# Combining weights of the last batch moved from among the experts to among the output's blocks, and four output blocks in column halves instead of five

## The chip, the cores and the metric

The kernel runs on one NeuronCore of one Trainium2 chip. A core has a matrix engine (TensorE, "PE" in the profile; its weight loads are "PEld"), a vector engine (VectorE, "DVE"), a scalar engine (ScalarE, "ACT"), GpSimd ("POOL"), and SyncE ("SP"), from which this kernel issues all its DMAs. The DMAs run on 16 DMA engines. The metric is the device time of one execution in microseconds; lower is better. The median of three runs is shown, and one more execution was taken with the hardware profiler.

## The reference

Causal attention with a decay per token (8 batches, 8 heads, 576 tokens, 64 channels a head) gives a matrix x of 4608 tokens by 512 channels. A soft mixture of experts follows: 32 slots, four for each of 8 experts. Cut to what matters here:

```python
logits = x @ phi                                   # 4608 x 32
d = exp(logits - logits.max(0)); d /= d.sum(0) + 1e-9    # over all tokens
slot_input = (d.T @ x).reshape(8, 4, 512)
for e in range(8):
    slot_out[e] = maximum(slot_input[e] @ w1[e], 0.0) @ w2[e]
c = exp(logits - logits.max(1)); c /= c.sum(1) + 1e-9    # over the 32 slots
out = c @ slot_out.reshape(32, 512)                # 4608 x 512
```

The weights d need every token's logits, so the experts can't start before the last batch's attention is done. The weights c, called combining weights here, need only their own token's logits, and they are needed only in the last line. Batches 0 to 6 have theirs made during the attention; this document is about those of batch 7 (`B - 1`, named `b` in the code).

## The kernel before, in words

The program is one long hand-ordered list. Every engine executes its own instructions in the order in which the Python code issues them, and semaphores hold an instruction back until its operands are ready. Nothing is reordered afterwards: a line of Python that stands earlier stands earlier in its engine's queue.

The attention takes the first 320 us or so. Then come, in this order:

1. The weights d of the last batch, and the slot inputs.
2. The experts, in the loop over `STEPS`. A step `(e, 0)` is expert e's first layer (`mlp1`, 32 matmuls, line 936) and `relu`; a step `(e, 4)` or `(e, 6)` is one half of its second layer (`mlp2`, line 973). The expert weights come from HBM in quarters of 512 KB each. 23 of the 64 quarters have a place of their own; the others go into memory that becomes free, so the weights stream in until near the end of the experts (line 128, function `wload`). For experts 4 to 7 the second layer is stored by output columns: steps `(e, 4)` give columns 0 to 255 of the slots' outputs, steps `(e, 6)` columns 256 to 511.
3. The output. `blocks(m, c)` makes block m, 512 tokens by the columns c: 8 matmuls of `cT` (combining weights, transposed) with `SO` (slot outputs, as a rounded part and a remainder), four copies from PSUM to a staging buffer, two on ACT and two on DVE (line 1053), and two DMAs to HBM from SP (line 1055). The first carries what ACT copied, the second what DVE copied. There are nine blocks. The first `FIRST` blocks are made in column halves, because columns 0 to 255 of the slot outputs are ready first: their blocks are written while `mlp2(e, 1)`, the last halves of the second layers, still run. A block in halves is four DMAs of 256 KB with runs of 1 KB in HBM; a whole block is two DMAs of 512 KB. `gathered`, `slots` and `halve` turn the sum of one column half of the expert outputs into `SO`.

The combining weights of batch 7 are made in these steps, which the change moves:

- `tokens(b, 0)`: the logits are turned to tokens-by-slots on PE (lines 457 and 458).
- `combine(b, 0)`: on DVE the maximum over the slots and the difference (lines 510 and 511); `combine(b, 1)`: the exponential on ACT (line 514); `combine(b, 2)`: on DVE the sum, the reciprocal and the product (lines 518 to 521).
- `split(3, 0)` and `split(3, 1)`: the rounded part on ACT (line 702) and the remainder on DVE (line 704), for batches 3 and 7 together.
- `cols(3, turn)`: five transposes on PE (line 712), and two casts on ACT into `cT` (line 718). They fill columns 864 to 1151 of `cT`, and block m reads columns 128 m to 128 m + 127, so the blocks 6, 7 and 8 need them.

PSUM banks are handed out in turn from a list named `ring` (function `turn`); before the second column half it has eight banks. The six staging buffers (`stage`) are used in turn too, one for each half block and two for a whole block.

Of the kernel before, what the change touches and what calls it, by code (L numbers as in the profile page):

```python
# [29 lines left out]
NQ = 8 * NE  # L30
QW = 1024
DEFER = 4
FIRST = 5

STEPS = (
    (0, 0), (1, 0), (2, 0), (3, 0), (0, 4), (0, 6), (1, 4), (1, 6), (4, 0), (5, 0), (2, 4), (2, 6), (3, 4), (3, 6),
# [36 lines left out]
def attn_softmoe(ctx: ExitStack, tc: tile.TileContext, qk, v, f, phi, w1, w2, cst, out):  # L73
# [86 lines left out]
    def batch(b):  # L160
        return 0 <= b < B
# [5 lines left out]
    def turn():  # L167
        ring.append(ring.pop(0))
        return ring[-1]
# [281 lines left out]
    def tokens(b, *ns):  # L451

        if not batch(b):
            return
        pm = turn() if b == B - 1 else scratch(False, f"tk{b}")
        for n in ns:
            nc.tensor.transpose(pm[:, 160 * n : 160 * n + 128], (LG, EX)[n][:, 0:128], ident)
            nc.tensor.matmul(pm[:, 160 * n + 128 : 160 * n + 160], (LX, EX[:, 128:256])[n], srep[:, 0:NS], start=True, stop=True)
        if 0 in ns:
            st["tok", b] = pm  # L460
            if b < B - 1:
                nc.tensor.transpose(pm[:, 160:192], st["mb", b][0:32, 1:2].broadcast_to([32, P]), ident[0:32, 0:32])
        if 1 in ns:
            nc.vector.tensor_copy(LD, pm[:, 160:320].rearrange("p (t s) -> p t s", t=NBLK))
# [36 lines left out]
    def combine(b, step):  # L501

        if not batch(b):
            return
        ce = ctok[:, b]
        if step == 0:

            lt = (TK if b < B - 1 else st["tok", b])[:, 0 : NBLK * NS].rearrange("p (t s) -> p t s", t=NBLK)
            sm = st["sm", b] = const.tile([P, 2, NBLK], F32, name=f"sm{b}", tag="sm", bufs=1)
            nc.vector.tensor_reduce(sm[:, 0], lt, axis=AX.X, op=ALU.max)  # L510
            nc.vector.tensor_tensor(ce, lt, wide(sm[:, 0]), op=ALU.subtract)
        elif step == 1:
            st["ce"] = turn()
            nc.scalar.activation(st["ce"][:, 0 : NBLK * NS].rearrange("p (t s) -> p t s", t=NBLK), ce, AF.Exp)
        else:
            sm, pm = st["sm", b], st["ce"]
            et, to = pm[:, 0 : NBLK * NS].rearrange("p (t s) -> p t s", t=NBLK), pm[:, NBLK * NS : NBLK * NS + NBLK]
            nc.vector.tensor_reduce(to, et, axis=AX.X, op=ALU.add)
            nc.vector.tensor_scalar_add(sm[:, 1], to, EPS)
            nc.vector.reciprocal(sm[:, 1], sm[:, 1])  # L520
            nc.vector.tensor_tensor(ce, et, wide(sm[:, 1]), op=ALU.mult)
# [174 lines left out]
    def split(b, *parts):  # L696

        if 0 in parts:
            CW[b] = tp.tile([P, NBLK, 2, 2, NS], F32R, name=f"cw{b}", tag="cw", bufs=2)
        hi, lo = (CW[b][:, :, :, r].rearrange("p t h s -> p h t s") for r in range(2))  # L700
        if 0 in parts:
            nc.scalar.copy(hi, ctok[:, b::4])
        if 1 in parts:
            nc.vector.tensor_tensor(lo, ctok[:, b::4], hi.bitcast(F32), op=ALU.subtract)

    def cols(b, bank):

        for lo, hi in ((0, 2), (2, 5)):
            pm = bank()
            for t in range(lo, hi):  # L710
                n = 128 if t < 4 else 64
                nc.tensor.transpose(
                    pm[:, 128 * (t - lo) : 128 * (t - lo) + n], CW[b][0:n, t].rearrange("p h r s -> p (h r s)").bitcast(F32), ident[0:n, 0:n]
                )
            yield
            at = (b * S + 128 * lo) // 2
            w = 128 if lo == 0 else 160
            nc.scalar.copy(cT[:, :, at : at + w], pm[:, 0 : 2 * w].rearrange("p (n r) -> p r n", r=2))
            yield


    for g in range(1, NG):
        h0, h1 = 2 * g, 2 * g + 1
        u0, u1 = h0 + 3, h0 + 4
        b, w = divmod(g - 4, NPAIR)
# [132 lines left out]
    b = B - 1  # L858
# [124 lines left out]
    for e, k in STEPS[:-4]:  # L983
        if k == 0:
            mlp1(e, 0, 1, 2, 3)
            relu(e)
        else:
            mlp2(e, k // 2 - 2)
        n = used + (2 if k else 4)
        wstream(*quarter[used : min(n, NRES)])  # L990
        used = n
        if (e, k) in ((2, 0), (4, 0), (6, 0), (4, 4)):
            own({(2, 0): 0, (4, 0): 2, (6, 0): 4, (4, 4): 6}[e, k])
        if (e, k) == (1, 0):
            tokens(b, 0)
            combine(b, 0)
        if (e, k) == (3, 0):
            combine(b, 1)
            combine(b, 2)
            split(3, 0, 1)  # L1000
        if (e, k) == (5, 0):
            for _ in cols(3, turn):
                pass
        if (e, k) == (1, 6):
            blank_h(4)
            blank_h(5)
        if (e, k) == (5, 0):
            late.close()
            sp = ctx.enter_context(tc.tile_pool(name="sp", bufs=1))
            so = sp.tile([P, DM], F32, name="so")  # L1010

            SO = [sp.tile([P, DM], F32R, name=f"SO{r}") for r in range(2)]
        if (e, k) == (3, 6):
            nc.scalar.copy(so, pv[0])
            blank_h(6)
            blank_h(7)

    half = [slice(256 * n, 256 * n + 256) for n in range(2)]
# [10 lines left out]
    def slots(n):  # L1029
        nc.tensor.matmul(pr[n], srep, so[:, half[n]], start=True, stop=True)  # L1030

    def halve(n):
        nc.scalar.copy(SO[0][:, half[n]], pr[n])
        nc.vector.tensor_tensor(SO[1][:, half[n]], pr[n], SO[0][:, half[n]].bitcast(F32), op=ALU.subtract)
# [3 lines left out]
    def blocks(m, c=slice(0, DM)):  # L1038

        w = c.stop - c.start  # L1040
        o = []
        for h in range(2):
            n, at = divmod(state[0], QW)
            o.append(stage[n % len(stage)][:, at : at + 2 * w].rearrange("p (r c) -> p r c", r=2))
            state[0] += 2 * w
        for n in range(2):
            pm = [turn()[:, 0:w] for _ in range(2)]
            for r in range(2):
                for h in range(2):
                    rows = slice(64 * h, 64 * h + 64)  # L1050
                    nc.tensor.matmul(pm[h], cT[rows, n, 128 * m : 128 * m + 128], SO[r][rows, c], start=(r == 0), stop=(r == 1))
            for h in range(2):
                copies[h](o[h][:, n], pm[h])
        for h in range(2):
            nc.sync.dma_start(outv[:, h, m, :, c], o[h])
# [7 lines left out]
    blocks(0, half[0])  # L1063
    mlp2(5, 1)
    blocks(1, half[0])
    blocks(2, half[0])
    mlp2(6, 1)
    blocks(3, half[0])
    mlp2(7, 1)
    gathered(1)  # L1070
    blocks(4, half[0])
    slots(1)
    halve(1)
    ring += [bank[1], po[1]]
    for m in range(FIRST):
        blocks(m, half[1])
    for m in range(FIRST, NT):
        blocks(m)

# [40 lines left out]
```

## Time and profile before

| | |
|---|---|
| median of 3 runs | 389.95 us (389.6 to 391.09) |
| profiled execution: its own time | 391.69 us |
| profiled execution: span of the profile | 390.0 us |
| PE busy | 370.0 us, 95% of the span |
| DVE busy | 297.4 us, 76% |
| ACT busy | 269.8 us, 69% |
| DMA: bytes moved | 93.72 MB, 240 GB/s over the span |
| HBM read and written | 63.93 MB and 9.73 MB |

All times in the views are microseconds from the start of the span. The profiled execution's own time is 1.69 us more than its span. A view of windows gives for each stretch of time how long each engine was busy in it, the clock granted to PE, the mean busy share of the 16 DMA engines (1.00 is all 16, and 0.06 is one of them; the records overlap a little, so that a full stretch can show 1.05), and the rate in GB/s. A row of the timeline with "SPq" is a DMA issue on SP: start, duration of the issue, line, and what is written from what. In the chain of waits the work that ended last is followed back through what released it.

### The profile page before, as it was taken

To read this page: it belongs to the slowest core of one execution; us is meant where nothing else is said; L and a number is where in the kernel's file an instruction comes from. 1 tells how busy PE (TensorE), PEld (TensorE's weight loads), DVE (VectorE), ACT (ScalarE), POOL (GpSimd) and SP (SyncE) were. 2 spreads that over 40 slices of the span, in tenths; PEclk is the share of its full clock that TensorE was granted. 3 is DMA by queue.
4 is the path that set the end of the run, shared out by engine and by line. 5 is a ranking of instruction groups with operands and counts; after the bars stand their busy time and mean duration, and the time that the engine had idled before them with its cause. 6 is when DMAs were issued, how large, how long until landed. Compare 5 with 4: busy or idle time off the path is not lost.

```text
span 390.0 us, 15261 instructions
## 1 busy us (share of the span) xinstructions
PE 370.0 (95%) x5891; PEld 328.6 (84%) x5891; DVE 297.4 (76%) x1161; ACT 269.8 (69%) x685; POOL 251.4 (64%) x339
## 2 busy tenths in 40 slices
PE   8989999999999999999999999999999989999960
PEld 7879999999999999999999999999999877444630
DVE  7787887989798979897988898889888734412651
ACT  8887787878787878787878787878776454010540
POOL 3769987878787878787878787878787721000000
PEclk9999999999999999999999999999999999999975
DMA  6876667767867777777777777777765999999898
GB/s 206 227 158 159 167 190 210 202 191 246 249 192 231 218 230 202 228 203 229 215 211 214 214 214 213 216 213 214 213 180 157 294 344 362 408 408 397 288 359 344
DMA packets 34120, 93.72 MB, mean 240 GB/s; under 512 B 4234, under 2 KB 10048, under 8 KB 34048
## 3 DMA queue, kind: packets, MB, share of 16 engines
q1 hardware_dynamic: 34048, 92.75, 76.4%
q8 instruction: 46, 0.75, 0.8%
q14 instruction: 26, 0.21, 0.2%
HBM read 63.93 MB, written 9.73 MB: 189 GB/s over the span
## 4 chain that ended last, share of the span: by engine, by line
PE 84%; DMA 5%; POOL 3%; DVE 2%; issue 2%; ACT 1%; DVEq 0%; SPq 0%; ACTq 0%; POOLq 0%
PE pv L313 23%; PE ring L280 14%; PE ring L281 12%; PE s L230 11%; PE pv L340 4%; PE pv L973 3%; PE lg L387 2%; PE ds L490 2%; PE ring L936 2%; PE pv L936 2%; DMA YA<-mr 2%; POOL WB L209 1%; DMA out<-p 1%; POOL YB L214 1%; PE pv L527 1%
## 5 line engine op out<-in xcount | busy, mean ns | idle before, releaser
L287 ACT ACTIVATE PTS<-ring 128x320 f32<-128x320 f32 (+2 forms) x256 | 118.1, 502 | 51.6 <-PE ring L281 40.1
L243 DVE CUSTOM_DVE_ANT_0 s<-s,mask 128x320 f32<-128x320 f32 (+4 forms) x320 | 138.5, 452 | 6.1 <-PE s L230 1.0
L280 PE MATMUL ring<-YA,WA 67*128 67x320 f32 (+9 forms) x384 | 119.6, 325 | 0.5 <-DMA YA<-mr 0.5
L281 PE MATMUL ring<-YB,WB 128*128 128x320 f32 (+4 forms) x384 | 110.7, 296 | 0.0
L313 PE MATMUL pv<-V,PTS 128*64 128x65 f32 x3200 | 101.9, 223 | 1.0 <-POOL PTS L295 0.7
L209 POOL TENSOR_TENSOR WB<-RAW,WB 64x576 fp32r<-64x576 f32 x64 | 91.0, 1422 | 16.2 <-ACT YA L188 5.6
L313 PEld LDWEIGHTS pv<-V,PTS 128*64 128x64 f32 x3200 | 97.1, 138 | 4.8 <-issue 1.2
L230 PE MATMUL s<-WA,YA 66*128 66x288 f32 (+9 forms) x384 | 100.3, 317 | 0.4 <-DVE MT L243 0.3
L214 POOL TENSOR_TENSOR YB<-RAW,YA 64x576 fp32r<-64x576 f32 x64 | 89.7, 1419 | 2.5
L280 PEld LDWEIGHTS ring<-YA,WA 67*128 67x128 f32 (+3 forms) x384 | 68.9, 181 | 6.0 <-issue 1.6
L281 PEld LDWEIGHTS ring<-YB,WB 128*128 128x128 f32 (+1 forms) x384 | 69.9, 182 | 0.0
L230 PEld LDWEIGHTS s<-WA,YA 66*128 66x128 f32 (+1 forms) x384 | 63.0, 191 | 5.1 <-DVE MT L243 0.5
L243 DVE DVE_READ_ACCUMULATOR2_ANT MT<- 128x1 f32 x372 | 52.5, 141 | 0.0
L298 POOL TENSOR_SCALAR_AFFINE_SELECT PTS<-PTS 128x128 f32<-128x128 f32 (+1 forms) x128 | 31.3, 265 | 30.3 <-ACT PTS L287 27.3
L295 POOL TENSOR_SCALAR_AFFINE_SELECT PTS<-PTS 128x384 f32<-128x384 f32 x64 | 33.3, 520 | 18.4 <-ACT PTS L287 14.3
L340 PE MATMUL pv<-cs,X 128*128 128x128 f32 x155 | 42.1, 273 | 0.6 <-DVE X L333 0.6
L183 ACT CAST WA<-RAW 64x576 fp32r<-64x576 f32 x64 | 40.0, 669 | 3.7 <-DMA RAW<-in_qk 2.8
L188 ACT CAST YA<-RAW 64x576 fp32r<-64x576 f32 x64 | 40.0, 669 | 0.4
L243 DVE CUSTOM_DVE_ANT_0 s<-s,mask,MT 128x288 f32<-128x288 f32 x62 | 32.6, 526 | 9.8 <-PE s L230 1.1
L333 DVE TENSOR_TENSOR X<-pv,rl 128x320 f32<-128x320 f32 (+1 forms) x65 | 31.5, 486 | 2.5 <-DMA YA<-mr 0.3
L376 ACT COPY XTS<-pv 128x128 f32<-128x128 f32 (+1 forms) x93 | 25.3, 307 | 1.1 <-PE pv L340 0.8
L340 PEld LDWEIGHTS pv<-cs,X 128*128 128x128 f32 x155 | 22.0, 142 | 1.4 <-DVE X L333 0.9
(215 smaller groups left out, 379.5 us busy)
## 6 DMA issues: line engine op xcount, KB each, us to landing
w<-in_w SPq DMA_DIRECT2D x44, 512.0 KB
RAW<-in_qk SPq DMA_DIRECT2D x31, 576.0 KB
V<-in_v SPq DMA_DIRECT2D x32, 325.0 KB
WB<-WA SPq DMA_DIRECT2D x31, 288.0 KB
YB<-YA SPq DMA_DIRECT2D x31, 288.0 KB
p<-in_w SPq DMA_DIRECT2D x7, 512.0 KB
out<-RAW SPq DMA_DIRECT2D x12, 256.0 KB
out<-p SPq DMA_DIRECT2D x5, 512.0 KB
```

The costliest lines, as they stand in the source:

```text
L183: nc.scalar.copy(WA[g % 3][0:64, S * h : S * h + S], RAW[g % 3][64:128, h])
L188: nc.scalar.copy(YA[g % 3][0:64, h, 64:640], RAW[g % 3][0:64, h])
L209: nc.gpsimd.tensor_tensor(t[0:64], RAW[g % 3][64:128, h], t[64:128].bitcast(F32), op=ALU.subtract)
L214: nc.gpsimd.tensor_tensor(YB[g % 2][64:128, h], RAW[g % 3][0:64, h], YA[g % 3][0:64, h, 64:640].bitcast(F32), op=ALU.subtract)
L230: nc.tensor.matmul(t[:, o : o + w], ya[0:m, h, 128 * blk : 128 * blk + 128], wa[0:m, j0 : j0 + w], start=True, stop=True)
L243: nc.vector.tensor_tensor_reduce(out=t[:, o : o + w], in0=t[:, o : o + w], in1=mask[:, m0 : m0 + w], scale=1.0, scalar=top if n == 3 else ...
L280: nc.tensor.matmul(o, wa[0:m, j0 : j0 + n], ya[0:m, h, 64 + i0 : 64 + i0 + w], start=True, stop=False)
L281: nc.tensor.matmul(o, wb[:, j0 : j0 + n], yb[:, h, i0 : i0 + w], start=False, stop=True)
L287: nc.scalar.activation(PT[i % 2][:, SEG_O[bank] : SEG_O[bank] + at], t[:, 0:at], AF.Exp, scale=0.125)
L295: nc.gpsimd.affine_select(d3, d3, pattern=[[0, 3], [1, 128]], compare_op=ALU.is_ge, fill=0.0, base=0, channel_multiplier=-1)
L313: nc.tensor.matmul(pvv[h][64 * u : 64 * u + 64, t, :], PT[h][:, at : at + 64], V[:, g % 2, c, 65 * h : 65 * h + 65], start=(c == 0), stop= ...
L340: nc.tensor.transpose(pm[:, 0:128], x[:, t, 128 * (p % 2) : 128 * (p % 2) + 128], ident)
```

## The change

The three insertions among the experts, `tokens(b, 0)` with `combine(b, 0)` after step (1, 0), `combine(b, 1)`, `combine(b, 2)` and `split(3, 0, 1)` after step (3, 0), and `cols(3, turn)` after step (5, 0), are taken out of the loop. They are put among the blocks of the second column half: `tokens` between `slots(1)` and `halve(1)`, the others one or two at a time between half blocks, and `cols` after the last of them. `FIRST` goes from 5 to 4, so that eight half blocks and five whole ones are made instead of ten and four. Among the half blocks of the first column half one half block instead of one or two stands between the parts of the second layer.

```diff
-FIRST = 5
+FIRST = 4
...
-        if (e, k) == (1, 0):
-            tokens(b, 0)
-            combine(b, 0)
-        if (e, k) == (3, 0):
-            combine(b, 1)
-            combine(b, 2)
-            split(3, 0, 1)
-        if (e, k) == (5, 0):
-            for _ in cols(3, turn):
-                pass
...
     blocks(0, half[0])
     mlp2(5, 1)
     blocks(1, half[0])
+    mlp2(6, 1)
     blocks(2, half[0])
-    mlp2(6, 1)
-    blocks(3, half[0])
     mlp2(7, 1)
     gathered(1)
-    blocks(4, half[0])
+    blocks(3, half[0])
     slots(1)
+    tokens(b, 0)
     halve(1)
     ring += [bank[1], po[1]]
-    for m in range(FIRST):
-        blocks(m, half[1])
+    blocks(0, half[1])
+    combine(b, 0)
+    combine(b, 1)
+    blocks(1, half[1])
+    combine(b, 2)
+    split(3, 0)
+    blocks(2, half[1])
+    split(3, 1)
+    blocks(3, half[1])
+    for _ in cols(3, turn):
+        pass
     for m in range(FIRST, NT):
         blocks(m)
```

How this moves the instructions shows at two places. The first is PE's queue among the experts, around step (5, 0) and the first part of expert 2's second layer. L936 is the first layer, L973 the second, `w_`, `p_` and `RAW_` are quarters of expert weights, `cw_` the combining weights of batches 3 and 7 before they are turned. A minus marks what stood there before and no longer does.

```order
 L936 MATMUL ring_150<-p_0_5527,EX 32x256 x4
 L936 MATMUL ring_150<-p_1_5528,EX 32x256 x4
 L936 MATMUL ring_150<-p_2_5529,EX 32x256 x4
 L936 MATMUL ring_150<-RAW_96,EX 32x256 x4
-L712 MATMUL ring_149<-cs,cw_5964 128x128 x2
-L712 MATMUL more_5732<-cs,cw_5964 128x128 x2
-L712 MATMUL more_5732<-cs,cw_5964 128x64
 L973 MATMUL pv_147<-p_5650,X_101 32x512 x2
 L973 MATMUL pv_147<-PTS,X_101 32x512 x2
```

The five transposes of `cols` leave the experts' matmuls; the transpose and the matmuls of `tokens` leave them in the same way four steps earlier.

The second place is DVE's queue in the output, from `gathered(1)` (the sum of the second column half into `so`) on. Before, with L1053 the copies of the blocks and L1034 the remainder in `halve(1)`:

```order
L1027 TENSOR_TENSOR so<-so,pv_147 128x256
L1053 COPY p_1_5363<-ring_151 128x256
L1053 COPY p_1_5363<-more_5732 128x256
L1034 TENSOR_TENSOR SO_6041<-ring_150,SO_6040 128x256
L1053 COPY p_0_5523<-lg_5653 128x256
L1053 COPY p_0_5523<-ring_151 128x256
L1053 COPY RAW_95<-more_5732 128x256
L1053 COPY RAW_95<-pv_147 128x256
L1053 COPY RAW_96<-lg_5653 128x256
L1053 COPY RAW_96<-ring_151 128x256
```

The same piece now, from the copies of the first half block of the second column half (lines of the output stand ten lower, so that L1043 is what L1053 was):

```order
L1043 COPY p_1_5363<-ring_149 128x256
L1043 COPY p_1_5363<-more_5733 128x256
L510 TENSOR_REDUCE sm_6227<-pv_148 128x5
L511 TENSOR_TENSOR ctok<-pv_148,sm_6227 128x160
L1043 COPY p_0_5523<-ring_150 128x256
L1043 COPY p_0_5523<-ring_151 128x256
L518 TENSOR_REDUCE lg_5653<-lg_5653 128x5
L519 TENSOR_SCALAR sm_6227<-lg_5653 128x5
L520 RECIPROCAL sm_6227<-sm_6227 128x5
L521 TENSOR_TENSOR ctok<-lg_5653,sm_6227 128x160
L1043 COPY RAW_95<-more_5732 128x256
L1043 COPY RAW_95<-lg_5653 128x256
```

Seven small operations of `combine` and `split` (the last of them, L704, follows these rows) now stand between the copies that the output DMAs wait for. On ACT the exponential and the rounded part stand between the copies in the same way.

## The prediction

> **What bounds the kernel now.** I read the chain of waits from its end, then the DMA share in narrow windows over the part that the change touches, then SP's issues there. In the chain of waits (start, duration, what it was) the experts are one unbroken piece of PE work, and the end is DMA:
>
> ```profile
> 333.90 1.86 PE pv L936 x32
> ...
> 364.67 1.00 PE pv L973 x16
> ...
> 371.66 3.33 DMA out<-RAW
> 375.11 0.70 DVE RAW L1053
> ...
> 376.98 4.31 DMA out<-p
> ```
>
> So PE sets the pace until about 366 us and the output's DMAs after it. That suggests that PE time saved among the experts is time saved. The windows correct this. After the stretch come busy times of PE, PEld, DVE, ACT and POOL, then PE's clock, the share of the 16 DMA engines and the rate:
>
> ```profile
> 358.00:360.00 2.00, 1.79 (x18) 0.75 (x15) 0.64 (x2) 0.37 (x1) 0.00 (x0) 1.00 1.00 391
> 360.00:361.00 1.00, 1.00 (x18) 0.69 (x22) 0.65 (x2) 0.65 (x2) 0.00 (x0) 1.00 0.73 291
> 361.00:362.00 1.00, 1.00 (x20) 0.59 (x14) 0.10 (x1) 0.01 (x1) 0.00 (x0) 1.00 0.30 123
> 362.00:362.20 0.20, 0.20 (x8) 0.20 (x4) 0.18 (x1) 0.20 (x1) 0.00 (x0) 1.00 0.10 41
> 362.40:363.70 1.30, 1.30 (x22) 0.80 (x20) 1.06 (x4) 0.88 (x3) 0.00 (x0) 1.00 1.04 345
> 364.00:366.80 2.80, 2.80 (x34) 1.71 (x34) 1.80 (x5) 1.29 (x4) 0.00 (x0) 1.00 1.03 341
> 367.00:367.40 0.40, 0.00 (x0) 0.00 (x0) 0.00 (x0) 0.37 (x1) 0.00 (x0) 1.00 0.07 23
> 370.00:376.00 6.00, 4.84 (x38) 3.17 (x38) 4.00 (x10) 3.57 (x9) 0.00 (x0) 1.00 1.03 345
> 380.00:388.00 8.00, 0.00 (x0) 0.00 (x0) 1.29 (x2) 1.07 (x2) 0.00 (x0) 0.50 1.02 406
> 388.00:388.60 0.60, 0.00 (x0) 0.00 (x0) 0.00 (x0) 0.00 (x0) 0.00 (x0) 0.50 0.83 321
> 388.70:390.00 1.30, 0.00 (x0) 0.00 (x0) 0.00 (x0) 0.00 (x0) 0.00 (x0) 0.50 0.00 0
> ```
>
> Up to 360 us all DMA engines carry expert weights. They don't finish together: the share falls to 0.73, 0.30 and 0.10, and 0.10 of 16 is still 1.6 engines at 362.2. From 362.4 they carry output. Half blocks go at 345 GB/s, whole ones at 406. There is one hole, 367.0 to 367.4, and its share is 0.07, which is 1.1 of 16: one engine works while the others wait. The DMA view of 364 to 366.5 us (queue, kind: packets, MB, share of 16 engines) shows what that engine had to carry beside its output:
>
> ```profile
> q1 hardware_dynamic: 858, 0.83, 101.1%
> q8 instruction: 1, 0.02, 2.4%
> ```
>
> One packet of program code took 2.4% of 16 engines over 2.5 us, which is 0.96 us of one engine. I infer that this is the late engine, and that it is also among the last with the weights; no row names the engine.
>
> A sum tests it. A DMA of 256 KB (0.262 MB) takes 0.262/345 GB/s = 0.76 us, one of 512 KB (0.524 MB) 0.524/406 = 1.29 us. From 362.2: 20 x 0.76 + 8 x 1.29 + 0.96 = 26.5, so the late engine would end at 388.7 if it never idled. The last bytes stand between 388.6 and 388.7. **The late engine is busy from the last weights to the last output byte**, and the end of the kernel is this sum. The others idle for about 0.27 + 0.70 + 0.18 = 1.2 us between 360 and 362.2 (the missing shares of the three rows) and 0.4 us in the hole, some 1.6 us, and that costs nothing if the late engine decides.
>
> **The change part by part.** *One block whole instead of in halves.* 1.049 MB go at 406 instead of 345 GB/s: 3.04 - 2.58 = 0.46 us less. It also saves SP two issues, which aren't the limit while DMA is.
>
> [...]
>
> *PE work taken from the experts.* These rows of PE's timeline (start, duration, instruction) hold it:
>
> ```profile
> 333.43 0.33 PE L457 MATMUL ring<-cs,LGM 128*128 128x128 f32 x1
> 333.60 0.31 PE L458 MATMUL ring<-cs,LGM 128*128 128x32 f32 x2
> 333.83 1.93 PE L936 MATMUL pv<-w,EX 128*32 128x256 f32 x32
> ...
> 345.32 0.44 PE L712 MATMUL ring<-cs,cw 128*128 128x128 f32 x2
> 345.60 0.58 PE L712 MATMUL more<-cs,cw 128*128 128x128 f32 x3
> 346.11 0.62 PE L973 MATMUL pv<-p,X 128*32 128x512 f32 x2
> ```
>
> From start to the next start, `tokens` held PE for 333.83 - 333.43 = 0.40 us and `cols` for 346.11 - 345.32 = 0.79. Everything behind them on PE comes 1.19 us earlier, the first output issue too:
>
> ```profile
> 360.98 4.24 SPq L1055 DMA_DIRECT2D out<-RAW  x6
> 365.31 4.87 SPq L1055 DMA_DIRECT2D out<-p  x6
> 370.28 4.33 SPq L1055 DMA_DIRECT2D out<-RAW  x6
> ```
>
> From 360.98 it moves to 359.8. Between the first issue and the full share in the windows lie about 1.3 us, so that output could flow at 361.1. Engines done with their weights would take it; the late one can't before 362.2. Worth, bounded: 0 if the late engine decides, 1.19 + 0.4 = 1.6 if the mean engine does (first output earlier, hole closed). I take 0, because the late engine's sum meets the end to 0.1 us. The weights don't come sooner either: their stream is at a share of 1.00 whatever PE does. The last weights are there at 362.2, and PE wants them about 363 in the changed kernel (today from 364.67 on, the chain's last row of PE), so they are close but not awaited.
>
> *The same work put among the blocks.* Its DVE and ACT operations, from where they are today:
>
> ```profile
> 333.97 0.32 DVE L510 TENSOR_REDUCE sm<-ring 128x5 f32<-128x160 f32 x1
> 334.32 0.33 DVE L511 TENSOR_TENSOR ctok<-ring,sm 128x160 f32<-128x160 f32 x1
> 334.76 0.31 ACT L514 ACTIVATE more<-ctok 128x160 f32<-128x160 f32 x1 [4.52 <-DVE ctok L511]
> 338.47 0.32 DVE L518 TENSOR_REDUCE more<-more 128x5 f32<-128x160 f32 x1
> 339.25 0.32 DVE L521 TENSOR_TENSOR ctok<-more,sm 128x160 f32<-128x160 f32 x1
> 339.60 0.46 ACT L702 CAST cw<-ctok 128x320 fp32r<-128x320 f32 x1 [4.54 <-DVE ctok L521]
> 340.09 0.49 DVE L704 TENSOR_TENSOR cw<-ctok,cw 128x320 fp32r<-128x320 f32 x1 [0.52 <-ACT cw L702]
> ```
>
> They form one chain that crosses between DVE and ACT: 0.7 us for L510 and L511, 0.3 for the exponential and 0.1 for the handover, 1.1 from 338.47 to 339.57 for L518 to L521 (two small ones between), 0.5 for L702, 0.5 for L704: 3.2 us, and for `cols` 0.8 on PE and about 0.8 on ACT (taken as two casts like L702). Behind them wait the copies of the second column half, and behind these SP, which issues in order. Do the DMAs run dry? Today the second half begins here:
>
> ```profile
> 368.34 0.42 DVE L1053 COPY p<-lg 128x256 f32<-128x256 f32 x1 [0.51 <-PE lg L1051]
> 368.68 0.41 DVE L1053 COPY p<-ring 128x256 f32<-128x256 f32 x1
> ```
>
> In the changed kernel this comes earlier by 1.19 us and by one half block of PE work (0.7, at 0.34 a DVE copy), so its copies end at about 369.1 - 1.9 = 367.2. `tokens` costs PE 0.4 there, but PE waits for `halve(1)` at that point (the 0.4 us window with PE at 0.00). By then eight half DMAs are issued, or ten with this one: enough for the late engine until 362.2 + 0.96 + 10 x 0.76 = 370.8. The chain then goes: L510 and L511 until 367.9, exponential until 368.3. The next half block waits on PE for the bank that `tokens` held, and its copies end about 369.0, in time for 370.8 (an issue needs 4.24/6 = 0.7 us and the way to the first byte as much again, so the copy must end by 369.4). That feeds the engine until 372.3. L518 to L521 last until 370.1, L702 until 370.6, the two ACT copies of the third half block until about 371.0; needed by 372.3 - 1.4 = 370.9. The fourth follows 0.7 us later. So the cover is just used up: cost 0 to 0.2, and I take 0. If the chain is 1 us longer, nearly all of that second is lost at the end. After it, `cols` and the whole blocks are ahead of the DMAs again: 1.4 us of copies (two of 0.70 us, as in the chain) for a block that drains in 2.6. I take these times as good to half a microsecond, so the cost's upper end is 0.9.
>
> *Sum.* -0.46 + 0 + 0 = -0.5 us. The profiled execution's span goes from 390.0 to 389.5, its own time from 391.7 to 391.2, and the median of the runs, 1.7 us below that execution, from 389.95 to **389.5**.
>
> [...]
>
> **The rivals.** (A) *The mean engine decides.* If the hole and the early idle shares come from late output and not from one late engine, the earlier start is worth up to 1.6: 389.95 - 0.46 - 1.6 = 387.9. For it speaks that PE leads the chain of waits until 367. Against it speak the share of 0.07, one engine, at 367 and the late engine's sum. (B) *The output runs dry in the combining chain.* Were none of it beside other work, 3.2 us of chain and 1.6 of `cols` would stand between half blocks, against a backlog at 367.2 of 370.8 - 367.2 = 3.6 less the 1.4 from copy to bytes, 2.2: 4.8 - 2.2 - 0.46 = +2.1, at 392.1. It decides from the point where the copies of the third half block end after 370.9. For it speaks that DVE and ACT work in order and cross five times; against it that PE and the copies of other halves run during most of the handovers. A mild form, up to 0.9 late, gives 389.5 to 390.4. (C) *The change does nothing:* half blocks drain more slowly not for their runs of 1 KB but because something else is on the chip's path until 378 us, so that a block gains nothing whole: 389.95. Against it: the rate steps from 345 to 406 just when the whole blocks begin, and the share is full on both sides.
>
> **How the numbers follow.** Forecast 0.60, A 0.11, B in full 0.05, mild B 0.16, C 0.08. About 0.5%, 1.95 us, is what a measurement of this kernel can tell from no change. Only A in nearly its full size passes it downwards (0.10, with what an unknown may add), and only B in full upwards (0.05), so 0.85 stay within. The range goes from nearly A, 388.0, to above mild B, 390.7; the three runs of before spread over 1.5 us themselves.
>
> **What would show it.** Right: SP's first output issue at about 359.8; the share near 1.0 from 362.4 on with at most a short hole at about one engine; 16 half DMAs at 345 GB/s and ten whole ones at 406; the last bytes about 0.5 us sooner. Against the late engine: last bytes 1 us or more sooner. For B: a hole in the DMA share between 370 and 374, with SP waiting for an ACT or DVE copy there. The forecast is wrong beyond its range if the code packet falls where it delays no one, or the last weights, which PE now wants within a microsecond of their coming, are awaited.

## The result, and the profile after

The changed kernel is slower by half a per cent.

| | median | lowest to highest | runs |
|---|---|---|---|
| before | 390.5 us | 389.6 to 391.42 us | 8 |
| changed | 392.66 us | 390.92 to 449.27 us | 8 |

The ratio is 1.0054, with a 95% interval of 1.0029 to 1.0079, so 1.1 to 3.1 us lost. Forecast was 389.5 us, with a range from 388.0 to 390.7.

Medians and ranges here and below are over all executions, but the ratios leave out those in a slower state of the chip, and since the execution profiled with this result was one of them (449.27 us at a granted clock of 0.748), the rows below come from the last experiment's execution of the same program, of 392.45 us around a span of 390.7.

Its windows, over the last batch's experts and the output. The columns are those of the windows in the prediction: busy time of PE, PEld, DVE, ACT and POOL, PE's clock, DMA share, GB/s.

```profile
358.00:362.00 4.00, 3.82 (x56) 1.79 (x48) 1.78 (x6) 1.57 (x6) 0.00 (x0) 1.00 1.02 391
362.00:377.00 15.00, 11.46 (x89) 9.30 (x87) 9.33 (x25) 7.81 (x21) 0.00 (x0) 0.77 0.79 270
377.00:385.00 8.00, 1.90 (x16) 1.36 (x12) 3.69 (x6) 2.84 (x6) 0.00 (x0) 0.82 1.02 405
```

The first two stretches in the kernel before:

```profile
358.00:362.00 4.00, 3.79 (x46) 2.03 (x44) 1.40 (x4) 1.03 (x4) 0.00 (x0) 1.00 0.76 299
362.00:377.00 15.00, 13.30 (x133) 8.96 (x130) 9.96 (x24) 8.73 (x24) 0.00 (x0) 0.97 0.98 324
```

Before, the DMA engines lost 4 x 0.24 = 0.96 us ahead of 362 us, between the weights and the output, and 15 x 0.02 = 0.3 behind it: 1.3 us in all. After, nothing is lost ahead of 362 us, since the output now starts early enough to fill that gap, but 15 x 0.21 = 3.15 us behind it. That is 1.9 us more. The 0.46 us of the one block more that goes whole takes it to 1.4, against the measured 1.1 to 3.1.

The two executions don't lie side by side without a shift, though. These are PE's last logits, which end the attention's stream of work, and the first layer of the first expert, before:

```profile
318.51 0.45 PE L387 MATMUL lg<-XTS,phis 128*32 128x144 f32 x8
320.33 0.70 PE L387 MATMUL lg<-XTS,phis 128*32 128x144 f32 x16 [1.36 <-issue]
...
329.84 1.93 PE L936 MATMUL pv<-w,EX 128*32 128x256 f32 x32
```

And after:

```profile
318.90 0.94 PE L387 MATMUL lg<-XTS,phis 128*32 128x144 f32 x24
...
328.66 1.93 PE L936 MATMUL pv<-w,EX 128*32 128x256 f32 x32
```

In the traced execution of the kernel before, PE stood idle for 1.36 us among the last logits, for nothing that the profile shows ("issue"), ahead of everything that the change touches. No trace of the experiments has so long an idle time there. That execution took 391.69 us, against medians of 390.0 to 390.5. So what happens behind the logits is best counted from the first expert's first layer: the output's first issue comes 31.14 us behind it before and 29.68 after (358.34 us, in a row below), 1.46 us earlier. Of the 2.64 us between the two issues in absolute time, 1.18 are not the change's, and some of the 0.96 us lost in the gap isn't the old order's either.

The loss is in five holes, each with its windows here (the share is the last number but one):

```profile
364.80:365.80 1.00, 0.71 (x7) 0.41 (x7) 0.42 (x1) 0.31 (x1) 0.00 (x0) 1.00 0.45 152
367.20:368.00 0.80, 0.53 (x8) 0.53 (x10) 0.21 (x1) 0.31 (x1) 0.00 (x0) 1.00 0.32 109
369.40:370.00 0.60, 0.12 (x2) 0.13 (x2) 0.57 (x3) 0.14 (x1) 0.00 (x0) 0.50 0.25 82
371.40:372.20 0.80, 0.65 (x4) 0.55 (x4) 0.80 (x3) 0.37 (x1) 0.00 (x0) 0.50 0.09 28
375.20:376.40 1.20, 1.20 (x13) 1.20 (x12) 1.20 (x3) 1.05 (x3) 0.00 (x0) 0.99 0.08 31
```

Each ends when the next block's output arrives, about 1.3 us (the last 0.9) behind its first issue on SP. The output's first issue, and the one that ends the third and the fourth hole, in the timeline:

```profile
358.34 4.93 SPq L1045 DMA_DIRECT2D out<-RAW  x6
...
368.68 0.53 SPq L1045 DMA_DIRECT2D out<-p  x1
...
370.95 0.53 SPq L1045 DMA_DIRECT2D out<-RAW  x1
```

What was late there are PE's matmuls of the half blocks. PE's waits between 361.5 and 378 us (who waited, for whom, us in total, times, longest):

```profile
PE lg L1041 <- DVE ctok L521: 1.3, 1, 1.3
PE pv L1041 <- DVE ctok L511: 1.2, 1, 1.2
PE pv L973 <- DMA w<-in_w: 0.6, 1, 0.6
```

L1041 are the matmuls of a block. They don't read `ctok`. They wait for L511 and L521 because these are the last readers of the two PSUM banks that `tokens` and the exponential took from the ring, and the half blocks are handed the same banks next. In the timeline, with the two operations of DVE:

```profile
362.76 0.64 PE L973 MATMUL pv<-w,X 128*32 128x256 f32 x8 [0.60 <-DMA w<-in_w]
...
367.09 0.33 DVE L511 TENSOR_TENSOR ctok<-pv,sm 128x160 f32<-128x160 f32 x1
367.47 0.38 PE L1041 MATMUL pv<-SO,cT 64*128 64x256 f32 x1 [1.24 <-DVE ctok L511]
...
369.50 0.32 DVE L521 TENSOR_TENSOR ctok<-lg,sm 128x160 f32<-128x160 f32 x1
369.88 0.58 PE L1041 MATMUL lg<-SO,cT 64*128 64x256 f32 x1 [1.27 <-DVE ctok L521]
```

The wait for the last weights at 362.2 to 362.8 us precedes the first hole, the change-over to the second column half the second, and the two waits for banks the third and the fourth. The fifth stands behind the end of the combining chain. The chain of waits, which before went from the half blocks straight to the output's DMAs, now runs through `split` (L704) and `cols` (L712):

```profile
371.05 0.49 DVE cw L704
...
371.68 0.66 PE ring L712 x2
372.33 0.72 PE more L712 x3
...
377.26 4.84 DMA out<-p
```

PE's clock has fallen to 0.50 by then. `cols` and the first whole block run at it (0.50 from 372 to 375 us): the first two transposes of `cols` take 0.66 us, among the experts they took 0.44.

### The profile page after: what moved, and what is told of

Same layout as the page of the kernel before. It is cut to its first block, busy times and chain, and to the rows that moved or that the text cites. A ratio compares the mean times of both kernels' runs of the same rounds, so it can differ in the third digit from the quotient of the medians.

```text
span 447.6 us, 15235 instructions
## 1 busy us (share of the span) xinstructions
PE 431.6 (96%) x5883; PEld 381.8 (85%) x5883; DVE 299.8 (67%) x1159; ACT 274.2 (61%) x683; POOL 250.8 (56%) x339
## 4 chain that ended last, share of the span: by engine, by line
PE 95%; DVE 2%; DMA 1%; issue 1%; DVEq 0%; ACT 0%; ACTq 0%
PE pv L313 27%; PE ring L280 14%; PE ring L281 13%; PE s L230 13%; PE pv L340 5%; PE pv L973 3%; PE lg L387 2%; PE ring L936 2%; PE ds L490 2%; PE pv L936 2%; PE pv L527 2%; PE ring L527 1%; PE pv L253 1%; PE ring L973 1%; DMA out<-p 1%; PE ring L1041 1%
## 5 line engine op out<-in xcount | busy, mean ns | idle before, releaser
L280 PE MATMUL ring<-YA,WA 67*128 67x320 f32 (+9 forms) x384 | 129.0, 348 | 0.0
L313 PE MATMUL pv<-V,PTS 128*64 128x65 f32 x3200 | 122.1, 245 | 0.3 <-ACT mr L262 0.3
L281 PE MATMUL ring<-YB,WB 128*128 128x320 f32 (+4 forms) x384 | 120.3, 320 | 0.0
L313 PEld LDWEIGHTS pv<-V,PTS 128*64 128x64 f32 x3200 | 116.8, 155 | 3.5 <-issue 2.5
L230 PE MATMUL s<-WA,YA 66*128 66x288 f32 (+9 forms) x384 | 113.8, 355 | 0.1
L280 PEld LDWEIGHTS ring<-YA,WA 67*128 67x128 f32 (+3 forms) x384 | 73.1, 192 | 7.4 <-issue 2.3
L230 PEld LDWEIGHTS s<-WA,YA 66*128 66x128 f32 (+1 forms) x384 | 69.6, 205 | 6.8 <-DVE MT L243 0.4
L281 PEld LDWEIGHTS ring<-YB,WB 128*128 128x128 f32 (+1 forms) x384 | 74.3, 194 | 0.1
L340 PE MATMUL pv<-cs,X 128*128 128x128 f32 x155 | 47.2, 306 | 0.2 <-DVE X L333 0.2
L328 DVE TENSOR_SCALAR rl<-pv 128x5 f32<-128x5 f32 x64 | 10.5, 165 | 46.3 <-PE pv L313 45.3
```

The source lines that it names most:

```text
L230: nc.tensor.matmul(t[:, o : o + w], ya[0:m, h, 128 * blk : 128 * blk + 128], wa[0:m, j0 : j0 + w], start=True, stop=True)
L280: nc.tensor.matmul(o, wa[0:m, j0 : j0 + n], ya[0:m, h, 64 + i0 : 64 + i0 + w], start=True, stop=False)
L281: nc.tensor.matmul(o, wb[:, j0 : j0 + n], yb[:, h, i0 : i0 + w], start=False, stop=True)
L313: nc.tensor.matmul(pvv[h][64 * u : 64 * u + 64, t, :], PT[h][:, at : at + 64], V[:, g % 2, c, 65 * h : 65 * h + 65], start=(c == 0), stop= ...
L340: nc.tensor.transpose(pm[:, 0:128], x[:, t, 128 * (p % 2) : 128 * (p % 2) + 128], ident)
```

## The experiments

Every run has the kernel before beside it on the same chip. Ratios are to that.

### Each half of the change alone, and the changed kernel once more

The changed kernel unaltered:

> The changed kernel once more, for a profile at PE's full clock and a tighter ratio (it was measured 0.5% slower, where 0.1% faster was forecast; the profile shown with it was taken at a granted clock of 0.75). If the combining chain starves the output (rival B), the ratio is 1.004 to 1.006, the last DMA bytes come about 2 us later than before, and there is a hole of 1 us or more in the DMA share between the half blocks of the second column half. If the loss lies before the output, the first output issue is not 1.19 us earlier than before (360.98 us in the trace of before). If the late engine alone decides, the ratio is 0.998 to 1.000 and the loss was noise.

Only four blocks in halves; the combining work stays among the experts:

```diff
-FIRST = 5
+FIRST = 4
...
     blocks(1, half[0])
+    mlp2(6, 1)
     blocks(2, half[0])
-    mlp2(6, 1)
-    blocks(3, half[0])
     mlp2(7, 1)
     gathered(1)
-    blocks(4, half[0])
+    blocks(3, half[0])
```

> The combining stays among the experts; only four blocks instead of five are made in halves, with one half block between the parts of the second layer. Theory of the prediction (one block faster by 0.46 us): ratio 0.9988. If starvation by the combining chain is the loss: the same 0.9988 or a little below 1. If the loss comes from having fewer half blocks ready while the second column half is summed (PE has nothing to hand out during that wait): ratio 1.001 to 1.003, and the DMA share's hole at the wait grows from 0.4 us to about 1.1 us.

Only the combining work moved; five blocks in halves as before:

```diff
-        if (e, k) == (1, 0):
-            tokens(b, 0)
-            combine(b, 0)
...
+    tokens(b, 0)
     halve(1)
...
+    for _ in cols(3, turn):
+        pass
+    blocks(4, half[1])
```

> The combining is moved among the blocks as in the change, but five blocks are made in halves as before. Theory of the prediction: 0.999 to 1.001 (late engine busy, nothing gained, nothing lost). If the combining chain starves the output: 1.003 to 1.007, since the backlog ahead of the chain is one half block larger than in the change, at most 0.7 us less loss than there. If the loss is that of the four blocks alone: 1.000.

| | median | ratio, 95% |
|---|---|---|
| changed | 393.58 us | 1.0070 (1.0043 to 1.0097) |
| four halves only | 390.36 us | 0.9998 (0.9986 to 1.0011) |
| moved only | 390.62 us | 1.0003 (0.9989 to 1.0016) |

Neither half costs anything; together they cost 0.7% here. So the loss lies in what the two do to each other, or elsewhere. Moved only has the same two waits of PE in the output (1.2 us for L511, 1.3 for L521) and comes out even.

The first trace of the changed kernel misled me. It shows its loss in the first 30 us, where the change alters nothing. The low parts of the second pair (POOL) and the clock, with the row of the first batch's logits:

```profile
24.90 1.40 POOL L209 TENSOR_TENSOR WB<-RAW,WB 64x576 fp32r<-64x576 f32 x1 [7.77 <-DMA WB<-WA]
```

```profile
24.00:26.00 2.00, 0.00 (x0) 0.00 (x0) 1.07 (x6) 1.95 (x5) 1.10 (x1) 1.00 0.17 40
28.00:30.00 2.00, 2.00 (x22) 1.66 (x19) 0.36 (x1) 0.00 (x0) 1.93 (x2) 0.50 0.60 124
```

```profile
L387 PE MATMUL lg<-XTS,phis x32: 286/286/310, 66.5 to 67.4; 128*32 128x144 f32 x32
```

In the kernel before the same POOL instruction starts at 22.28 us, and the logits at 63.3:

```profile
22.28 1.39 POOL L209 TENSOR_TENSOR WB<-RAW,WB 64x576 fp32r<-64x576 f32 x1 [4.92 <-DMA YB<-YA]
...
L387 PE MATMUL lg<-XTS,phis x32: 286/286/310, 63.3 to 64.2; 128*32 128x144 f32 x32
```

With the low parts 2.6 us late PE stands idle at 24 to 26 us (0.00), its clock falls to 0.50, and 3.2 us are lost. The DMA view of 20 to 28 us holds one packet of program code (q8), which the kernel before fetched ahead of 20 us; that it held up the copies is a guess that no row confirms. From the last batch's logits to the last byte, this execution was no slower than before (69.4 us from 321.1 on, before 70.2 from 318.5 on), or 0.3 us slower when it is counted from the first expert's first layer, without the idle time of before. I took "chance at the start" as a theory (S) beside rival B, the starving output.

### The start: a load moved, a program shifted, another trace

One POOL instruction more, ahead of the output:

```diff
     gathered(0)
+    nc.gpsimd.memset(one, -1.0)
     mlp2(4, 1, 0)
```

> The changed kernel with one POOL instruction more, an unneeded memset of a 128x4 tile that is no longer read, just ahead of the output's blocks (POOL is idle there). Everything before 350 us is the changed kernel's, word for word. Theory L (the loss is chance in how this one program's code packets fall at the start, and nothing that the change does): back to the time before, ratio 0.998 to 1.002, with the first batch's logits at 63 to 64 us. Theory S (the first code packet of TensorE falls late, at 21 us, on a DMA engine that is to bring the second pair's rows, for a reason that this memset leaves alone): still 1.005 to 1.008, the first logits at 66 us. Theory T (the loss is in the combining chain among the blocks): still 1.005 to 1.008, with the first logits at 63 to 64 us and a longer way from the last batch's logits to the last byte than the 70.1 us of before.

The load of the fourth pair moved behind two copies, in the changed kernel and in the one before:

```diff
-    load_qk(3)
     dup_k(1)
     dup_q(1)
+    load_qk(3)
```

> The changed kernel with one DMA moved in the program's start: the 576 KB load of the fourth pair's queries and keys is issued behind the two copies of the second pair's rows (WB<-WA, YB<-YA), for which POOL and then TensorE wait at 22 to 27 us, instead of ahead of them. Theory S (those copies are late because a code packet falls on an engine whose queue is full): with little ahead of them they land some 2 us earlier whatever the packet does, the first batch's logits come at 62 to 63.5 us, and the time is that of the next run, the kernel before with the same move, within 0.3%, and less than 1.002 of the kernel before. Theory L gives the same, since any other program would do. Theory T: the 0.6% stays between this run and the next.

> The kernel before with the same move of one DMA. All theories: 0.5 to 1 us sooner if POOL's wait of 4.9 us at 17 to 22 us shortens and TensorE's 0.5 us behind it goes, or no change; ratio 0.997 to 1.001. It is the base for the run with the changed kernel. If the moved load is then late for its own reader, POOL's low parts at 30 us, both lose the same.

The changed kernel again:

> The changed kernel once more, for another trace. Theory S: the ratio is 1.005 to 1.008 again, the first code packet is again at 21 us, POOL waits for WB<-WA until 24.9 us, and the first logits stand at 66 us. If the trace shows the first logits at 63 to 64 us and the time is still long, S falls, and the loss is elsewhere in the program.

| | median | ratio, 95% |
|---|---|---|
| changed, one POOL instruction more | 391.68 us | 1.0031 (1.0009 to 1.0053) |
| changed, load moved | 398.98 us | 1.0214 (1.0163 to 1.0265) |
| before, load moved | 395.40 us | 1.0073 (1.0037 to 1.0110) |
| changed, again | 391.71 us | 1.0024 (1.0000 to 1.0047) |

The first and the last settle it. The first logits of their traced executions start at 62.9 and 62.8 us, half a microsecond earlier than before. The first of these executions took 392.02 us all the same. The second took 390.50, the least of its ten, but from the first expert's first layer to the end of the span it needed 61.8 us, where the kernel before needed 60.1. The output's stretches of the one with the POOL instruction (last logits at 318.3 us) are those of the changed kernel, with a share of 0.78 and a loss of 3.3 us:

```profile
358.00:362.00 4.00, 3.51 (x49) 1.54 (x40) 1.48 (x5) 1.29 (x4) 0.00 (x0) 1.00 1.02 386
362.00:377.00 15.00, 11.31 (x84) 9.32 (x82) 9.24 (x24) 7.31 (x19) 0.00 (x0) 0.77 0.78 268
```

So theory S falls as the whole cause; the late start of the first trace was an accident of that execution. How often it happens, and whether it is part of why the ratio was 1.0070 in one comparison and 1.0024 in another, these runs don't tell.

The moved load failed in its purpose: by the ratios it cost 2.9 us in the kernel before and 8.4 in the changed one, for a reason none of my expectations had. In the changed kernel with the load moved, PE's longest wait from 18 to 50 us and the windows after it:

```profile
PE s L230 <- DMA YA<-mr: 2.1, 1, 2.1
```

```profile
24.00:28.00 4.00, 2.67 (x28) 2.40 (x29) 1.40 (x6) 2.09 (x5) 3.80 (x3) 0.68 0.29 91
28.00:32.00 4.00, 4.00 (x37) 3.45 (x35) 2.80 (x12) 0.66 (x3) 3.15 (x3) 0.50 0.81 158
32.00:36.00 4.00, 4.00 (x21) 3.94 (x21) 2.21 (x10) 1.85 (x5) 0.52 (x1) 0.54 0.70 226
36.00:40.00 4.00, 4.00 (x65) 3.73 (x66) 3.69 (x16) 3.66 (x10) 2.91 (x6) 1.00 0.01 3
```

The 576 KB are now issued 1.5 us ahead of a tiny transfer (the row maxima, `YA<-mr`), which PE waits 2.1 us for; that they hold it up is read from this order, since no row follows the packets. Then the clock is 0.50 for most of the time to 36 us. The first logits of that run come at 68.1 us, instead of 63.8 in the execution of the changed kernel shown above. Since the two kernels with the moved load differ in how far this went (first logits at 68.1 and 73.0), they say nothing on the change.

### The banks, the clock and the columns

The two banks of the chain set aside until their last readers have been issued (`ring.sort` puts the bank last in the ring):

```diff
     combine(b, 0)
+    ring.sort(key=lambda t: t is st["tok", b])
     combine(b, 1)
     blocks(1, half[1])
     combine(b, 2)
+    ring.sort(key=lambda t: t is st["ce"])
```

> The changed kernel, with the two PSUM banks that the combining chain holds (the tokens' and the exponential's) put last in the ring behind each one's last reader, so that no half block waits for them. Theory B (the output runs dry in the combining chain, since TensorE's next half blocks wait for the chain's banks: 1.23 us for L511 and 1.31 us for L521 in two traces of the changed kernel, and the TensorE clock falls to 0.50 after them): both waits go, the holes at 7, 9.5 and 11.5 us behind the first output issue close or shrink, the clock stays up longer, what the 16 engines stand idle in the output falls from 2.3 to 3.6 us to 1 to 2, and the time by 1 to 1.5 us, to 0.999 to 1.002 of the kernel before. Theory S (only chance at the start): nothing changes but by the start, 1.002 to 1.007. A remaining hole is expected where `cols` waits for the chain's end.

Ten unneeded matmuls in PE's waits, into the unused half of a bank:

```diff
     combine(b, 1)
+    hold(3, -2)
     blocks(1, half[1])
     combine(b, 2)
     split(3, 0)
+    hold(5)
     blocks(2, half[1])
     split(3, 1)
     blocks(3, half[1])
+    hold(2)
```

> The changed kernel with ten unneeded 128x184 matmuls where TensorE waits in the combining chain: three ahead of the second half block of the second column half, five ahead of the third, two ahead of `cols`. Theory B with the clock as its larger half: the granted clock stays at 1.00 from 366 to 376 us instead of 0.50 from 370.5 on, the whole blocks' matmuls take 0.39 us instead of 0.62, the holes at 13.5 and 17.5 us behind the first issue (0.13 to 0.33 of the engines) close, and the time falls by 0.7 to 1.2 us, to 1.000 to 1.003. Theory B with the waits alone: the clock stays, but the time doesn't move (1.002 to 1.005).

The banks set aside, and `cols` ahead of block 6 instead of block 4:

```diff
-    for _ in cols(3, turn):
-        pass
     for m in range(FIRST, NT):
+        if m == 6:
+            for _ in cols(3, turn):
+                pass
         blocks(m)
```

> As the run with the two banks set aside, and `cols` (five transposes and two casts) moved behind two of the whole blocks, ahead of block 6, the first that reads these columns. TensorE then waits for no step of the chain among the half blocks. Theory B: the idle of the engines in the output falls to that of the kernel before, 0.4 to 0.9 us, TensorE's clock stays at 1.00, and what the change was made for is left: 0.46 us for the block that goes whole and up to 1.2 us for the earlier first output, so 388.3 to 389.8 beside 390.2 (0.996 to 0.999). If the late DMA engine and not the mean one decides, only the 0.46 us shows: 0.998 to 1.000. Theory S: no difference from the changed kernel.

| | median | ratio, 95% |
|---|---|---|
| banks set aside | 390.36 us | 0.9999 (0.9983 to 1.0014) |
| matmuls in the waits | 393.92 us | 1.0090 (1.0063 to 1.0116) |
| banks set aside, `cols` late | 390.14 us | 0.9995 (0.9972 to 1.0017) |

Two lines that change only which bank is handed out next bring the time back to that of before: the ratio is 0.9999, where that of the unaltered changed kernel was 1.0024 to 1.0070 in its four comparisons. PE's waits from 355 to 380 us and the output's stretch with the banks set aside:

```profile
PE pv L973 <- DMA w<-in_w: 1.8, 4, 0.6
PE more L712 <- DVE cw L704: 0.7, 1, 0.7
PE ring L1041 <- ACT p L1043: 0.3, 1, 0.3
PE lg L1041 <- DVE ctok L521: 0.2, 1, 0.2
```

```profile
362.00:377.00 15.00, 12.82 (x104) 10.07 (x104) 10.66 (x27) 8.89 (x23) 0.00 (x0) 0.89 0.88 306
```

The wait for L511 is gone, that for L521 went from 1.3 to 0.2 us, and the share rose from 0.79 to 0.88: 15 x 0.12 = 1.8 us lost instead of 3.15 (last logits at 318.4 us). What stays are the weights' waits, 1.8 us in all (the execution of the changed kernel shown above has 0.8 over the same stretch), and the 0.7 us at `cols`. With `cols` two blocks later the latter goes too, and the share is 0.92:

```profile
362.00:377.00 15.00, 13.45 (x98) 9.20 (x98) 10.27 (x25) 9.14 (x23) 0.00 (x0) 0.89 0.92 323
```

The matmuls in the waits kept the clock at 1.00 all through, as was meant, and made things worse:

```profile
366.71 1.20 PE L1049 MATMUL more<-cs 128*128 128x184 f32 x6 [0.64 <-DVE p L1043]
...
369.23 1.82 PE L1049 MATMUL ring<-cs 128*128 128x184 f32 x10 [0.64 <-DVE p L1043]
```

```profile
362.00:377.00 15.00, 11.63 (x102) 9.42 (x100) 7.91 (x23) 6.52 (x19) 0.00 (x0) 1.00 0.73 246
```

The three matmuls stand as six in the trace and took 1.20 us, the five as ten and took 1.82, and each group had to wait for a bank itself. PE's own time in this stretch is on the path. So a full clock doesn't make up for it; how much the half clock alone costs the changed kernel, this run can't tell, since it changed the time as well as the clock. Another trace bears on it, that of "changed, again" above. Its clock over these 15 us is 0.89, just as with the banks set aside, but the two waits of 1.2 and 1.3 us for the banks are there, and its share is lower:

```profile
362.00:377.00 15.00, 11.94 (x94) 9.50 (x90) 10.09 (x25) 8.75 (x23) 0.00 (x0) 0.89 0.83 288
```

So at the same clock the waits go with a loss of 2.6 us against 1.8 in this stretch. The half clock lasted about twice as long in the execution of 392.45 us (0.77), and from the first expert's first layer to the end that one needed only 0.3 us more.

### Five blocks in halves again, and a pair on one chip

The last kernel, with `FIRST` at 5:

```diff
-FIRST = 4
+FIRST = 5
```

> The run with `cols` behind two whole blocks and the chain's banks set aside, but with five blocks in halves as before the change, not four. If the output needs the cover of the fifth half block (theory B: with ten half DMAs issued by the time the halves change over, the switch and the chain pass without a hole), the engines' idle falls to 0.5 to 1 us and the earlier first output is left as a gain, less the 0.46 us that the fifth block costs in halves: 388.5 to 389.7 (0.996 to 0.999). If the four blocks were not short of cover once the banks were free, it is 0.4 us slower than the run with four: 390.0 to 390.6 (1.000 to 1.001).

> The changed kernel again, beside the other on one chip. Theory B (two waits for banks and the hole that each leaves in the output, some 2 us more idle of the engines than before, less 0.46 us): 1.002 to 1.005, first output issue 39.5 to 39.8 us behind the last batch's logits, PE waiting 1.2 to 1.3 us for L511 and for L521, the last byte 70 to 71 us behind the logits. If chance in the start is the larger part, as in its first trace: 1.006 to 1.008 and the first batch's logits at 66 us.

| | median | ratio, 95% |
|---|---|---|
| five halves, banks set aside, `cols` late | 389.01 us | 0.9974 (0.9959 to 0.9990) |
| changed, again | 392.02 us | 1.0054 (1.0031 to 1.0077) |

This version beats both kernels, the one before by 1.0 us (interval 0.4 to 1.6). PE's waits in it, and its stretches (last logits at 318.5 us, as before):

```profile
PE ring L1041 <- ACT RAW L1043: 0.6, 2, 0.3
PE more L1041 <- DVE ctok L521: 0.2, 1, 0.2
```

```profile
358.00:362.00 4.00, 4.00 (x60) 2.26 (x48) 2.05 (x7) 1.87 (x6) 0.00 (x0) 1.00 1.00 377
362.00:377.00 15.00, 13.17 (x102) 9.14 (x98) 11.05 (x28) 8.74 (x24) 0.00 (x0) 0.89 1.01 350
```

The share is full from the weights on, although the clock is 0.89 as in the two runs above. PE doesn't wait for the last weights in this execution. One half block more stands ahead of them than in the changed kernel, but that alone isn't why: moved only has the same order there, and PE waited 0.8 us.

Set beside each other, with one traced execution for each row: the time that the DMA engines lost over 19 us of the output (358 to 377 us, but from 360.5 us on for the first trace of the changed kernel and from 361.5 for moved only, whose experts start later), the time from the first expert's first layer to the end of the span, PE's waits for the last weights, and the median of all executions.

| kernel | lost, us | first layer to end, us | waits for weights, us | median, us |
|---|---|---|---|---|
| five halves, banks set aside, `cols` late | 0 | 58.9 | 0 | 389.01 |
| banks set aside, `cols` late | 1.2 | 59.9 | 0.6 | 390.14 |
| four halves only | 0.9 | 60.0 | 0 | 390.36 |
| before | 1.3 | 60.1 | 0 | 390.04 to 390.52 |
| changed, first trace | 1.8 | 60.5 | 0 | 393.58 |
| moved only | 1.2 | 61.0 | 0.8 | 390.62 |
| banks set aside | 1.8 | 61.4 | 1.8 | 390.36 |
| changed, again | 2.7 | 61.8 | 1.1 | 391.71 |
| changed, one POOL instruction more | 3.3 | 62.1 | 1.1 | 391.68 |
| changed, last trace | 3.15 | 62.1 | 0.8 | 392.02 |
| matmuls in the waits | 4.05 | 63.2 | 0.6 | 393.92 |

The medians follow the first two columns, with one clear exception. The first trace of the changed kernel has both waits for banks, and yet needed only 0.3 us more than before; it lost its time at the start, and PE didn't wait for weights in it. So the waits for banks cost most where the last weights are late too, and when these come, seen from PE, differs between executions. How much of the changed kernel's loss is the banks' alone the traces don't tell. That the banks are needed for it rests on the medians of the run that sets them aside, and that the cover of the fifth half block matters on moved only, which has the same waits and no loss.

## Why the prediction was wrong

**The step that failed** is the one on which the rest was built: "The late engine is busy from the last weights to the last output byte, and the end of the kernel is this sum." From it came both the worth of 0 for the earlier output and the cover for the combining chain.

- *First output issue at about 359.8 us.* Right in kind, and larger: counted from the first expert's first layer it comes 1.46 us earlier instead of the 1.19 worked out. That it came as early as 358.34 us is also luck of the baseline, since the trace that the prediction read had 1.36 us of idle time of PE ahead of the experts, which the changed kernel's doesn't have.
- *The earlier output is worth 0, because the late engine's sum meets the end to 0.1 us.* Wrong. The last kernel has the same five blocks in halves as the kernel before and moves the same bytes, and its output starts as early as the changed one's. By the medians it ends 1.0 us sooner, and in its trace the engines' share is 1.00 and 1.01 where the kernel before has 0.76 and 0.98. By the late engine's sum that couldn't be. Rival A, "the mean engine decides", priced the earlier start and the hole at up to 1.6 us, and the traces have 0.9 us (four halves only) to 1.3 us (before) of lost time to gain. That the sum fitted so well was a coincidence, or the late engine is late only where output isn't there to fill the others; no row names an engine, so this stays open. The packet of program code, which the prediction made the cause of the lateness, isn't enough for it: the last kernel's output has such a packet too (1.7% of 16 engines over 363 to 366.5 us, which is 0.95 us of one engine), and its share is full.
- *One block whole saves 0.46 us.* The rates hold: 405 GB/s in the whole blocks (377 to 385 us), and 350 in the last kernel's full stretch, most of which is half blocks. The saving doesn't show: four halves only measures 0.9998, with an interval that just reaches it, and with the chain's waits gone, five halves are 1.1 us faster than four by the medians (the intervals overlap). A block in halves is not only a slower DMA but also cover, since it can be issued while the second layers still run.
- *The combining chain costs 0 to 0.2 us, at most 0.9.* Its times came out right, by luck. I had L511 done at 367.9 and measured 367.4; L521 done at 370.1, measured 369.8; the third half block's copies at 371.0, measured 371.1. But the output started 1.5 us earlier than forecast, and the chain, seen from there, came 1 us later than forecast (L511 done 9.1 us behind the first issue instead of 8.1), with 0.8 us of waits for weights ahead of it; in the first trace, without these waits, it came 8.1 us behind. What was wrong is when the engines need them. I had ten half DMAs last until 370.8 for the late engine. But the output had started early and the engines, all of them, had taken it: the share is down to 0.45 at 365 us. There was no backlog to cover the chain. I also saw the bank that `tokens` holds, and gave the half block behind it its wait, but not the second one, for the bank of the exponential, which costs as much (1.3 us).
- *The last weights "are close but not awaited".* Wrong: PE waited 0.60 us for one of them, and 0.6 to 1.8 us in all in seven of the nine traces with the combining work moved that the table has; in the two with it among the experts it never waited. The text named this among the things that would break the forecast.
- *Rival B at 392.1 us* comes out nearest, with medians of 391.7 to 393.6. The place differs: its hole was to be at 370 to 374 us behind SP waiting for copies, and the holes run from 365 to 376 us behind PE waiting for banks. Its condition, copies of the third half block that end after 370.9, was met by 0.2 us. I gave it 0.05 in full because I read that condition against the wrong backlog.

PE's clock was 0.50 in the windows at 369 and 371 us, beside two waits of 1.2 and 1.3 us for banks. But at the same clock of 0.89 over 15 us the execution with the waits lost more (2.6 us) than the one with the banks set aside (1.8 us), so the clock isn't the whole of the loss. How much of it the clock makes stays open.

## What to carry to other kernels

Work that is put into a pipeline's idle engines also takes the pipeline's buffers: look who gets the same PSUM bank next, since a wait for a bank that somebody else's chain holds doesn't show in any data dependency (here two waits, 1.2 and 1.3 us), and changing the order in which banks are handed out can be the whole repair (here the ratio went to 0.9999 from 1.0024 to 1.0070). Before a stall is costed at nothing because a queue is full, work out what has drained from the queue by then in the changed kernel, not in the one before. A sum that meets the end to 0.1 us in one trace is not yet a mechanism; an independent run that removes the supposed cause is worth more. And a difference between two traces is not all the change's: before it is explained, look for idle time that one of them has upstream of the change.

## What the runs showed of the hardware

- With the load moved, 2.1 us in which PE waited for a small DMA were followed by a granted clock of 0.50 for most of the time to 36 us (0.68, 0.50 and 0.54 in the three windows of 4 us from 24 us on), and the first logits came at 68.1 us, 4.3 us later than in an execution of the changed kernel without the move. An estimate from the mean clocks of the rows, taking each as made up of 1.00 and 0.50, gives how long the half clock lasted: (15 x 0.11)/0.5 = 3.3 us in the output with the banks set aside, (15 x 0.23)/0.5 = 6.9 us in the changed kernel and (4 x 0.32 + 4 x 0.50 + 4 x 0.46)/0.5 = 10.2 us with the load moved. In the last case PE shows busy all the time (4.00 of 4.00) in the two windows from 28 to 36 us, at clocks of 0.50 and 0.54.
- With one 576 KB load issued 1.5 us ahead of a transfer of 2.5 KB on the same queue, PE waited 2.1 us for the small one.
- Executions of one program differ in their first 30 us: the wait of POOL for two copies took 5.1 us in one execution of the changed kernel and 7.8 in another, and the first logits came at 63.8 and 66.5 us.
